# Carrying the fixed instruction order of a sink-window attention kernel through the first four feed-forward steps

## The chip, the cores and the metric

The kernel is one program on one NeuronCore of a Trainium2 chip. The metric is device time in microseconds (us), the median over runs. The engines are named as in the profile: PE (TensorE matmuls), PEld (its weight loads), DVE (VectorE), ACT (ScalarE), POOL (GpSimd) and SP (SyncE, which here only issues DMAs). Each engine works through its own queue in order and waits there for semaphores of the others.

## What is computed

The inputs are q, k, v of shape (2, 8, 768, 64), and two pairs of feed-forward weights, all fp32.

```python
keep = (pos[None, :] < n_sink) | ((rel >= 0) & (rel < window))
a = softmax(where(keep, scale * q @ k.T, -1e9));  x = (a @ v), heads joined: (1536, 512)
h = x @ moe_w_in;   x = softplus(h) @ moe_w_out
h = x @ moe2_w_in;  out = (h * clip(h + 3, 0, 6) / 6) @ moe2_w_out
```

The first feed-forward part is called w1 ("softplus"), the second w2 ("hard"); w_in is 512 x 2048 and w_out 2048 x 512.

## The kernel before

**Attention** (`banded_attention`) handles 12 groups of 128 query rows, each in two quads of four heads. Iteration n is quad n % 2 of group n // 2. In it PE computes the scores `s`; DVE adds the mask and takes the row maximum (`xs`, `mx`, L481); ACT takes the exponential (`P`, L486); PE transposes P (`pt`, L511; the 16 sink columns as `pts`, L502, which POOL has gathered into `PS`, L491); DVE or ACT copies the transposed block to SBUF (`PT`); and PE multiplies with v (`o`, L553, sinks at L538). The second half of a quad's transposes and products is done one iteration later. When both quads of a group are through, DVE takes the reciprocal of the row sums (`rs`, L561 and L562) and scales the output (`x`, `normalise`, L567). PE turns x (`xtr`, `turn_x`, L575), and ACT and DVE write it as a high and a low fp32r part into `xT` (`store_hi` L578, `store_lo` L582). PSUM tile `o` has one buffer.

**Feed-forward** (`Ffn.run`) is a list of 96 steps: (w1, w2) x 3 blocks of 512 tokens x 16 chunks of 128 hidden units. Step s has `stage_a`: 12 matmuls of 128x512 into PSUM tile `h` (L143), then the activation. For w1 that is five ACT instructions, a POOL subtraction `u`, two DVE instructions (L172 and L173), a last ACT copy `g` (L174) and a POOL subtraction (L175). Two steps behind it comes `stage_b`: 12 matmuls that add into the four tiles `y` (L200). The h tiles have three buffers (pool `psa`, shared with the scores), so the products of step s+3 wait until L173 of step s has read its h.

**Weights.** The inputs arrive as 8-byte words, and each 128 x 512 half of a weight chunk must be converted: three DVE instructions (L95, L98, L101), one ACT (L105), one POOL (L106). In the attention the middle value lies in SBUF, in the feed-forward part in a PSUM tile `m`. The 64 halves are taken in a fixed sequence; of w1's 32, HALVES lists the iterations of the attention that end with one conversion (10 of them), and `filler` spreads the other 22 over steps 2 to 14 of the first block. Since step 2 is the first whose activation is not already in the attention code, its filler asks for five halves at once.

**What sets the order.** The tile framework's scheduler chooses the order of each engine's queue from the dependencies. Around the attention loop stands `with in_order(tc)`: it ties every instruction to the one before it on the same engine, in the order of the code. Steps 0 and 1 of w1 are in part written inside that loop: `ffn.products` at n = 24 and 25, `ffn.activate` in the same iterations, and after n = 25 the loop turns and stores the last group. What comes later is free, and the scheduler may put free instructions between the tied ones.

```python
            if NQ <= n < NQ + 2:
                ffn.activate("w1", "softplus", 0, n - NQ, lambda: None)
            if n in HALVES:
                w.half()
```

```python
            if key == first and blk == 0:
                self.w.upto(w0 + ((32 - w0) * (s + 1) + 14) // 15)
```

Of the kernel before, what the change touches and what calls it, by code (L numbers as in the profile page):

```python
# [8 lines left out]
F32 = mybir.dt.float32  # L9
# [5 lines left out]
ALU = mybir.AluOpType  # L15
# [7 lines left out]
SLOTW = P + SK  # L23
SLOTPOS = (0, 2, 1, 3)
TB = 2
HALVES = (5, 7, 9, 11, 13, 15, 17, 19, 21, 23)
WARM = 22


class in_order:  # L30
# [87 lines left out]
class Ffn:  # L118
# [103 lines left out]
    def run(self, specs, out, nblk, w0, pool2):  # L222


        steps = [(key, kind, blk, c) for (key, kind, _, _) in specs for blk in range(nblk) for c in range(16)]
        n = len(steps)
        first = specs[0][0]

        def filler(s):
            key, kind, blk, c = steps[s]  # L230
            if key == first and blk == 0:
                self.w.upto(w0 + ((32 - w0) * (s + 1) + 14) // 15)
            else:
                for _ in range(1 + s % 2):
                    if self.w.coming or self.w.todo:
                        self.w.half()

        for s in range(n + 2):
            if s < n:
                self.stage_a(*steps[s], lambda: filler(s))  # L240
            i = s - 2
            if i < 0 or i == n - 2:
                continue
            key, kind, blk, c = steps[i]
            for j in range(4):
                if i == n - 1:

                    with self.tc.issue_after(last.ins) if j else ExitStack():
                        self.stage_b(*steps[n - 2], j)
                last = self.stage_b(key, kind, blk, c, j)  # L250
# [10 lines left out]
def sink_window_attention_ffn_kernel(  # L261
# [46 lines left out]
    with ExitStack() as body:  # L308
        big = body.enter_context(tc.tile_pool(name="big", bufs=1))
        xT = big.tile([P, 2, 4, NT], F32R, name="xT")  # L310
        w = Weights(nc, body.enter_context(tc.tile_pool(name="wt", bufs=1)), 4)
        NW0 = 8
        wpool0 = body.enter_context(tc.tile_pool(name="wp0", bufs=1))
        psa = body.enter_context(tc.tile_pool(name="psa", bufs=3, space=PSUM))
        ffn = Ffn(tc, xT, w, psa)
        order = [(0, 0)] + [x for c in range(15) for x in ((c + 1, 0), (c, 1))] + [(15, 1)]
        for c, io in order[: 2 * NW0]:
            w.add("w1", c, io, w1_in, w1_out, wpool0)

        ffn.tmp = body.enter_context(tc.tile_pool(name="tmp", bufs=1))  # L320
        with ExitStack() as att:
            banded_attention(att, tc, qT, kT, v, ident, NSv, Wv, xT, psa, ISQ, w, ffn)

        wpool1 = body.enter_context(tc.tile_pool(name="wp1", bufs=1, reuse_waits="tile"))
        ffn.psy = body.enter_context(tc.tile_pool(name="psy", bufs=1, space=PSUM, reuse_waits="tile"))
        w.psum = body.enter_context(tc.tile_pool(name="psw", bufs=1, space=PSUM, reuse_waits="tile"))
        for c, io in order[2 * NW0 :]:
            w.add("w1", c, io, w1_in, w1_out, wpool1)
        w.fetch()
        homes = {x: wpool0 if n < 2 * NW0 else wpool1 for n, x in enumerate(order)}  # L330
        ffn.run(specs, out, NT // 512, w.done, lambda c, io: homes[c, io])


    rv = nc.values_load(near[0:1, 0:1], min_val=0, max_val=1)
    with tc.If(rv < 1):
        nc.scalar.preload_act_table_set("natural_log_exp_and_others")
        with ExitStack() as body:
            big = body.enter_context(tc.tile_pool(name="gbig", bufs=1))
            xT = big.tile([P, 2, 4, NT], F32R, name="gxT")
            with ExitStack() as att:  # L340
                dense_attention(att, tc, qT, kT, v, ident, NSv, Wv, xT, ISQ)
            w = Weights(nc, body.enter_context(tc.tile_pool(name="gwt", bufs=1)), 4)
# [8 lines left out]
            ffn.run(specs, out, NT // 512, 4, lambda c, io: wpool)  # L351


def banded_attention(ctx, tc, qT_d, kT_d, v, ident, NSv, Wv, xT, psa, isq, w, ffn):
# [236 lines left out]
    with in_order(tc):  # L591
        fetch(0)
        z = one.tile([P, 512], BF16, name="z")
        nc.vector.memset(z, 0.0)
        nc.gpsimd.iota(rmc, pattern=[[-1, P]], base=0, channel_multiplier=1, allow_small_or_imprecise_dtypes=True)
        nc.gpsimd.iota(col, pattern=[[1, P]], base=0, channel_multiplier=0, allow_small_or_imprecise_dtypes=True)

        nc.gpsimd.iota(ph, pattern=[[0, 2], [-MAXSINK, 4]], base=4 * MAXSINK, channel_multiplier=1)
        nc.vector.tensor_single_scalar(out=ph, in_=ph, scalar=3 * MAXSINK, op=ALU.bitwise_and)
        nc.vector.tensor_single_scalar(out=owner, in_=ph.rearrange("p a c -> p (a c)"), scalar=0, op=ALU.is_equal)  # L600
        nc.vector.memset(m_one[:, :, P:SLOTW], hid)
        nc.vector.tensor_scalar(out=tB, in0=rmc, scalar1=0.0, scalar2=hid, op0=ALU.is_lt, op1=ALU.mult)
        spare = ps1.tile([P, 512], F32, tag="tr", name="spare")
        keep_busy(WARM)
        masks(0)
        fetch(1)
        fetch_sinks(0)
        fetch(2)
        keep_sinks(0)
        for n in range(NQ + 3):  # L610
            g, quad = divmod(n, 2)
            new, old = n < NQ, 0 <= n - 1 < NQ
            done = (n - 3) // 2 if n % 2 and n >= 3 else None
            if new:
                scores(n)
            if n == NQ:
                ffn.products("w1", 0, 0)
            if done is not None:
                normalise(done)
            if n == NQ + 1:  # L620
                ffn.products("w1", 0, 1)
            if n < 3:
                keep_busy(6)
            if old:
                transposes(n - 1, 1)
                transposes(n - 1, 2)
            if new:
                exps(n, 0)
            if n >= 4 and n % 2 == 0:
                store_lo(n // 2 - 2)  # L630
            if old:
                copies(n - 1, 1)
                copies(n - 1, 2)
                apply_v(n - 1, 0)
            if new:
                exps(n, 1)
                transposes(n, 0)
            if done is not None:
                turn_x(done)
            if old:  # L640
                apply_v(n - 1, 1)
                apply_v(n - 1, 2)
                if n % 2 == 0:
                    inverse((n - 1) // 2)
            if new:
                copies(n, 0)
            if done is not None:
                store_hi(done)
            if quad == 1 and g + 1 < NG:
                keep_sinks(g + 1)  # L650
                if g % NB == 0:
                    own_sinks(g // NB)
                if g == 3:
                    fetch_sinks(1)
                if g + 3 < NG:
                    fetch(g + 3)
                if g == 0:
                    w.fetch()
            if n < 3:
                masks(n + 1)  # L660
# [119 lines left out]
```

## Time and profile before

| what | value |
|---|---|
| runs, device us | 656.67 median of 3 (655.88 to 656.87) |
| profiled execution, device us | 656.36 |
| its span, first to last instruction | 654.5 us, mean granted clock 0.994 |
| PE busy | 637.3 us, 97% of the span |
| DVE, ACT, POOL busy | 337.4, 334.1, 215.0 us |
| chain that ended last | PE 92%, issue 4% |

The profiled execution's own time is 1.9 us more than its span. The attention takes about the first 118 us, the w1 part the stretch to about 380 us, w2 the rest. PE is busy throughout both feed-forward parts; the one long idle stretch of PE lies where the attention ends.

### The profile page before, as it was taken

The page shows a single profiled execution, that of the slowest core. Times are in us where ns is not written, and L with a number is a line of the kernel's source. Part 1 is how long each engine was busy: PE and PEld are TensorE (multiplying, and loading weights), DVE is VectorE, ACT ScalarE, POOL GpSimd, SP SyncE. Part 2 cuts the span into 40 slices and gives each one's busy share as a digit, 9 for nine tenths or more (in the row PEclk, how much of TensorE's full clock was granted, in tenths as well). Part 3 has the DMA queues.
Part 4 walks back from the last instruction along what each step waited for, and adds up shares of the span by engine and source line. Part 5 has one row for each costly group of instructions (what it writes and reads, how often), then busy time and mean ns, then how long its engine had stood idle before and what let it go on. Part 6 is the DMA issues. An engine that isn't in the chain of part 4 may idle for free.

```text
span 654.5 us, 8810 instructions
## 1 busy us (share of the span) xinstructions
PE 637.3 (97%) x3160; PEld 525.3 (80%) x3160; DVE 337.4 (52%) x693; ACT 334.1 (51%) x707; POOL 215.0 (33%) x197
## 2 busy tenths in 40 slices
PE   8999999779999999999999999999999999999996
PEld 4888788668888888888888888888888888888884
DVE  4778987799932412225699999222232222322221
ACT  3767776568775756667688774222222222222221
POOL 1023122388965444444688993000000000000000
PEclk9999999979999999999999999999999999999999
DMA  7835552750000000003565640000010000100001
GB/s 231 259 126 158 163 178 88 246 182 1 1 0 2 0 1 1 2 1 91 179 200 179 212 137 33 1 1 0 2 65 1 1 0 1 64 1 0 1 1 70
DMA packets 38143, 47.07 MB, mean 72 GB/s; under 512 B 2121, under 2 KB 30793, under 8 KB 38089
## 3 DMA queue, kind: packets, MB, share of 16 engines
q1 hardware_dynamic: 37400, 46.15, 22.3%
q8 instruction: 27, 0.44, 0.3%
q10 hardware_dynamic: 688, 0.26, 0.2%
q14 instruction: 28, 0.22, 0.1%
HBM read 43.26 MB, written 3.15 MB: 71 GB/s over the span
## 4 chain that ended last, share of the span: by engine, by line
PE 92%; issue 4%; POOL 1%; ACT 1%; DVE 1%; POOLq 0%; DVEq 0%
PE h_w L143 40%; PE y_w L200 40%; PE o L553 4%; PE s L469 2%; PE pt L511 2%; PE spare L589 2%; PE o L538 1%; POOL w_w L106 1%; PE xtr L575 0%; DVE PT L524 0%; ACT P L486 0%; POOL ring L446 0%; POOL PS L491 0%; PE pts L502 0%; DVE xs L481 0%
## 5 line engine op out<-in xcount | busy, mean ns | idle before, releaser
L143 PE MATMUL h_w<-xT,w_w 128*128 128x512 f32 x1152 | 283.3, 391 | 7.6 <-DVE e_w L173 7.6
L143 PEld LDWEIGHTS h_w<-xT,w_w 128*128 128x128 f32 x1152 | 217.1, 189 | 53.7 <-DVE e_w L173 7.9
L200 PE MATMUL y_w<-g_w,w_w 128*128 128x512 f32 x576 | 142.4, 389 | 0.0
L200 PE MATMUL y_w<-w_w,g_w 128*128 128x512 f32 x576 | 138.9, 389 | 0.0
L200 PEld LDWEIGHTS y_w<-w_w,g_w 128*128 128x128 f32 x576 | 108.0, 188 | 23.2 <-ACT g_w L180 0.4
L200 PEld LDWEIGHTS y_w<-g_w,w_w 128*128 128x128 f32 x576 | 108.1, 188 | 22.5
L106 POOL TENSOR_TENSOR w_w<-t_w,w_w 128x512 fp32r<-128x512 f32 x64 | 83.0, 1297 | 47.0 <-ACT w_w L105 46.6
L179 DVE SCALAR_TENSOR_TENSOR h_w<-e_w,h_w 128x512 f32<-128x512 f32 x48 | 33.4, 695 | 89.0 <-ACT e_w L177 89.0
L177 ACT ACTIVATE e_w<-h_w 128x512 f32<-128x512 f32 x48 | 28.7, 599 | 96.4 <-PE h_w L143 94.6
L175 POOL TENSOR_TENSOR g_w<-e_w,g_w 128x512 fp32r<-128x512 f32 x48 | 62.2, 1297 | 47.1 <-ACT g_w L174 45.6
L181 DVE SCALAR_TENSOR_TENSOR g_w<-h_w,g_w 128x512 fp32r<-128x512 f32 x48 | 33.2, 691 | 83.2 <-ACT g_w L180 83.2
L180 ACT ACTIVATE g_w<-h_w 128x512 fp32r<-128x512 f32 x48 | 28.7, 598 | 90.4 <-PE y_w L200 90.1
L169 POOL TENSOR_TENSOR u_w<-u_w,e_w 128x512 f32<-128x512 f32 x48 | 62.1, 1294 | 31.9 <-ACT u_w L168 31.9
L486 ACT ACTIVATE P<-xs,mx 128x272 f32<-128x272 f32 (+1 forms) x96 | 47.4, 494 | 34.7 <-DVE mx L481 34.6
L172 DVE SCALAR_TENSOR_TENSOR h_w<-h_w,r_w 128x512 f32<-128x512 f32 x48 | 33.4, 697 | 59.0 <-ACT r_w L170 58.7
L173 DVE TENSOR_TENSOR e_w<-h_w,u_w 128x512 f32<-128x512 f32 x48 | 33.0, 688 | 33.9 <-POOL u_w L169 33.7
L165 ACT ACTIVATE e_w<-h_w 128x512 f32<-128x512 f32 x48 | 28.3, 592 | 42.4 <-PE h_w L143 36.3
L105 ACT ACTIVATE w_w<-t_w 128x512 fp32r<-128x512 f32 x64 | 40.1, 626 | 17.9 <-DVE t_w L101 17.2
L553 PE MATMUL o<-v,PT 128*128 128x64 f32 x352 | 45.0, 271 | 1.6 <-DVE PT L524 1.6
L553 PEld LDWEIGHTS o<-v,PT 128*128 128x128 f32 x352 | 42.7, 191 | 2.8 <-DVE PT L524 2.5
L95 DVE TENSOR_SCALAR m_w<-raw_w 128x512 int32<-128x512 int32 x54 | 37.4, 693 | 8.1 <-DMA raw_w<-in_moe_w_in_dram 3.9
L174 ACT ACTIVATE g_w<-e_w 128x512 fp32r<-128x512 f32 x48 | 30.0, 624 | 20.1 <-DVE e_w L173 15.6
(80 smaller groups left out, 523.8 us busy)
## 6 DMA issues: line engine op xcount, KB each, us to landing
raw_w<-in_moe_w_out_dram SPq DMA_DIRECT2D x32, 512.0 KB, 4.4
raw_w<-in_moe_w_in_dram SPq DMA_DIRECT2D x32, 512.0 KB, 4.8
v<-in_v_dram SPq DMA_DIRECT2D x12, 256.0 KB, 5.1
out_dram<-o SPq DMA_DIRECT2D x12, 256.0 KB, 2.1
q<-in_q_dram SPq DMA_DIRECT2D x11, 256.0 KB, 3.5
ring<-in_k_dram SPq DMA_DIRECT2D x11, 256.0 KB, 3.8
ring<-in_k_dram ACTq DMA_DIRECT2D x2, 128.0 KB, 6.1
q<-in_q_dram SPq DMA_DIRECT2D x2, 128.0 KB, 6.0
```

The source lines that it names most:

```text
L95: nc.vector.tensor_scalar(out=m, in0=hi, scalar1=3, scalar2=0x3FFFFFF8, op0=ALU.logical_shift_left, op1=ALU.bitwise_and)
L105: nc.scalar.activation(wt[:, 0, :], t.bitcast(F32), AF.Copy)
L106: nc.gpsimd.tensor_tensor(out=wt[:, 1, :], in0=t.bitcast(F32), in1=wt[:, 0, :].bitcast(F32), op=ALU.subtract)
L143: nc.tensor.matmul(h, wt[:, ws, kk * P : (kk + 1) * P], xT[:, xs, kk, t0 : t0 + 512], start=(n == 0), stop=(n == 11),)
L169: nc.gpsimd.tensor_tensor(out=u, in0=u, in1=e, op=ALU.subtract)
L172: nc.vector.scalar_tensor_tensor(out=h, in0=h, scalar=0.0, in1=r, op0=ALU.max, op1=ALU.add)
L175: nc.gpsimd.tensor_tensor(out=glo, in0=e, in1=ghi.bitcast(F32), op=ALU.subtract)
L179: nc.vector.scalar_tensor_tensor(out=h, in0=e, scalar=6.0, in1=h, op0=ALU.min, op1=ALU.mult)
L181: nc.vector.scalar_tensor_tensor(out=glo, in0=h, scalar=1.0 / 6.0, in1=ghi.bitcast(F32), op0=ALU.mult, op1=ALU.subtract)
L200: ins = nc.tensor.matmul(y, lhsT, rhs, start=(c == 0 and n == 0), stop=(c == 15 and n == 2))
L486: nc.scalar.activation(dst, xs, AF.Exp, scale=-1.0, bias=s["mx"][:, h : h + 1], accum_out=s["sum"][:, h : h + 1])
L553: nc.tensor.matmul(s["o"][:, h, :], t[:, o : o + P], st[gg]["v"][:, h, :], start=(k == 0 and (i <= 1 or hh == 0)), stop=(k == len(blocks) ...
```

## The change

The `in_order` block now also holds steps 0 to 3 of the feed-forward part (FIXED = 4), and their filler does nothing. `run` is cut in two calls, 0 to FIXED inside the block and the rest outside it. Twelve halves are converted in the attention: iterations 20 and 22 are added to HALVES, which then has every iteration from 19 to 23. The other 20 w1 halves are spread over steps 4 to 14. `normalise` and `activate` of the last group and of step 0 now come in iteration 24 (`n == NQ`), with normalise first; step 1's activation moves out of the loop into `run`. The rest of the loop is only indented less. Cut to its core:

```diff
-HALVES = (5, 7, 9, 11, 13, 15, 17, 19, 21, 23)
+HALVES = (5, 7, 9, 11, 13, 15, 17, 19, 20, 21, 22, 23)
+FIXED = 4
...
+    def filler(self, s):
+        key, kind, blk, c = self.steps[s]
+        if s < self.first_free:
+            return
+        if key == self.specs[0][0] and blk == 0:
+            if self.w0 is None:
+                self.w0 = self.w.done
+            n, of = s + 1 - self.first_free, 15 - self.first_free
+            self.w.upto(self.w0 + ((32 - self.w0) * n + of - 1) // of)
...
-        with ExitStack() as att:
-            banded_attention(att, tc, qT, kT, v, ident, NSv, Wv, xT, psa, ISQ, w, ffn)
...
-        ffn.run(specs, out, NT // 512, w.done, lambda c, io: homes[c, io])
+        ffn.begin(specs, out, NT // 512, FIXED, lambda c, io: homes[c, io])
+        with in_order(tc):
+            with ExitStack() as att:
+                banded_attention(att, tc, qT, kT, v, ident, NSv, Wv, xT, psa, ISQ, w, ffn)
...
+            w.fetch()
+            ffn.run(0, FIXED)
+        ffn.run(FIXED, 1000)
...
-            if done is not None:
-                normalise(done)
             if n == NQ + 1:
                 ffn.products("w1", 0, 1)
+            if done is not None and n < NQ:
+                normalise(done)
...
-            if NQ <= n < NQ + 2:
-                ffn.activate("w1", "softplus", 0, n - NQ, lambda: None)
+            if n == NQ:
+                normalise(NG - 1)
+                ffn.activate("w1", "softplus", 0, 0, lambda: None)
```

Line numbers of the changed kernel are larger, by 1 in the feed-forward code and by 12 in the attention. In the rows below, h_w1_0_c is the h tile of step c, y_w1_0_j one of the four y tiles, xtr_11 the turned output of the last group, and the last number of a name is only a counter.

PE, from the products of step 1 on, before:

```order
L143 MATMUL h_w1_0_1_1667<-xT_83,w_w1_1_0_635 128x512 x12
L143 MATMUL h_w1_0_2_1715<-xT_83,w_w1_2_0_896 128x512 x12
L143 MATMUL h_w1_0_3_1808<-xT_83,w_w1_3_0_1112 128x512 x11
L575 MATMUL xtr_11_1680<-ident_59,x_11_1665 128x128 x4
L143 MATMUL h_w1_0_3_1808<-xT_83,w_w1_3_0_1112 128x512
L143 MATMUL h_w1_0_4_1857<-xT_83,w_w1_4_0_1361 128x512 x12
L200 MATMUL y_w1_0_0_1792<-g_w1_0_0_1651,w_w1_0_1_764 128x512 x3
```

and now:

```order
L144 MATMUL h_w1_0_1_1685<-xT_83,w_w1_1_0_635 128x512 x12
L587 MATMUL xtr_11_1698<-ident_59,x_11_1669 128x128 x4
L144 MATMUL h_w1_0_2_1733<-xT_83,w_w1_2_0_896 128x512 x12
L201 MATMUL y_w1_0_0_1760<-g_w1_0_0_1671,w_w1_0_1_764 128x512 x3
L201 MATMUL y_w1_0_1_1764<-g_w1_0_0_1671,w_w1_0_1_764 128x512 x3
L201 MATMUL y_w1_0_2_1768<-g_w1_0_0_1671,w_w1_0_1_764 128x512 x3
L201 MATMUL y_w1_0_3_1772<-g_w1_0_0_1671,w_w1_0_1_764 128x512 x3
L144 MATMUL h_w1_0_3_1776<-xT_83,w_w1_3_0_1112 128x512 x12
L144 MATMUL h_w1_0_4_1815<-xT_83,w_w1_4_0_1361 128x512 x12
```

The turning of the last group moved from behind 35 product matmuls to right behind step 1's, and the y products of step 0 moved ahead of the products of steps 3 and 4. Behind step 4 come y of step 1, the products of step 5, y of step 2 and the products of step 6.

DVE, behind the scaling x of the last group, before (further conversions follow between the third row and the last three, 14 instructions in all):

```order
L567 TENSOR_TENSOR x_11_1665<-o_11_1574,rs_11_1648 128x512
L95 TENSOR_SCALAR m_w1_4_1_1739<-raw_w1_4_1_1240 128x512
L98 SCALAR_TENSOR_TENSOR m_w1_4_1_1739<-raw_w1_4_1_1240,m_w1_4_1_1739 128x512
...
L172 SCALAR_TENSOR_TENSOR h_w1_0_1_1667<-h_w1_0_1_1667,r_w1_0_1_1688 128x512
L101 SCALAR_TENSOR_TENSOR t_w1_6_1_1778<-raw_w1_6_1_1746,m_w1_6_1_1779 128x512
L172 SCALAR_TENSOR_TENSOR h_w1_0_2_1715<-h_w1_0_2_1715,r_w1_0_2_1730 128x512
L173 TENSOR_TENSOR e_w1_0_1_1687<-h_w1_0_1_1667,u_w1_0_1_1689 128x512
L582 TENSOR_TENSOR xT_83<-xtr_11_1680,xT_83 128x4x128
```

and now:

```order
L579 TENSOR_TENSOR x_11_1669<-o_11_1592,rs_11_1666 128x512
L173 SCALAR_TENSOR_TENSOR h_w1_0_0_1632<-h_w1_0_0_1632,r_w1_0_0_1673 128x512
L174 TENSOR_TENSOR e_w1_0_0_1672<-h_w1_0_0_1632,u_w1_0_0_1674 128x512
L594 TENSOR_TENSOR xT_83<-xtr_11_1698,xT_83 128x4x128
L96 TENSOR_SCALAR m_w1_5_1_1839<-raw_w1_5_1_1429 128x512
L99 SCALAR_TENSOR_TENSOR m_w1_5_1_1839<-raw_w1_5_1_1429,m_w1_5_1_1839 128x512
L102 SCALAR_TENSOR_TENSOR t_w1_5_1_1838<-raw_w1_5_1_1429,m_w1_5_1_1839 128x512
L173 SCALAR_TENSOR_TENSOR h_w1_0_1_1685<-h_w1_0_1_1685,r_w1_0_1_1721 128x512
L96 TENSOR_SCALAR m_w1_7_0_1849<-raw_w1_7_0_1497 128x512
L174 TENSOR_TENSOR e_w1_0_1_1720<-h_w1_0_1_1685,u_w1_0_1_1722 128x512
```

Four conversion instructions stand ahead of the read that frees step 1's h tile, where 15 did. From the L594 row to the read that frees step 3's h tile (the L174 row of step 3) there are 28 DVE rows, both included: the store, seven activation instructions and twenty of conversions.

DVE in the attention, between iterations 20 and 21 (x_9 is the scaled output of group 9), before:

```order
L561 TENSOR_SCALAR rs_9_1417<-sum_9_1242 128x8
L562 RECIPROCAL rs_9_1417<-rs_9_1417 128x8
L567 TENSOR_TENSOR x_9_1431<-o_9_1326,rs_9_1417 128x512
L481 ISA xs_21_0_1440,mx_10_1367<-s_21_0_1423,m_even_120 128x272
L481 ISA mx_10_1367 128x1
```

and now:

```order
L573 TENSOR_SCALAR rs_9_1417<-sum_9_1242 128x8
L574 RECIPROCAL rs_9_1417<-rs_9_1417 128x8
L96 TENSOR_SCALAR t_w1_3_1_1422<-raw_w1_3_1_1003 128x512
L99 SCALAR_TENSOR_TENSOR t_w1_3_1_1422<-raw_w1_3_1_1003,t_w1_3_1_1422 128x512
L102 SCALAR_TENSOR_TENSOR t_w1_3_1_1422<-raw_w1_3_1_1003,t_w1_3_1_1422 128x512
L579 TENSOR_TENSOR x_9_1440<-o_9_1326,rs_9_1417 128x512
L493 ISA xs_21_0_1449,mx_10_1367<-s_21_0_1432,m_even_120 128x272
L493 ISA mx_10_1367 128x1
```

A conversion now stands ahead of the scaling and of the next scores; between iterations 22 and 23 it is the same. On SP, the DMAs of two raw halves (6_1 and 8_0) stood ahead of the loads of group 3; they now stand behind the attention's loads, in the order of their use.

## Rows read from the trace of the kernel before

**Rows 1.** The page's engine table, whole span: busy time (share), count.

```profile
PE 637.3 (97%) x3160; PEld 525.3 (80%) x3160; DVE 337.4 (52%) x693; ACT 334.1 (51%) x707; POOL 215.0 (33%) x197
```

**Rows 2.** Stretches: length, busy (count) by engine, granted PE clock, DMA share, GB/s.

```profile
140.00:640.00 500.00, 500.00 (x2208) 414.01 (x2207) 226.96 (x342) 240.37 (x428) 177.43 (x140) 1.00 0.12 39
60.00:80.00 20.00, 18.68 (x153) 15.86 (x153) 18.16 (x64) 14.46 (x50) 5.83 (x8) 1.00 0.55 169
131.00:133.00 2.00, 0.00 (x0) 0.00 (x0) 1.55 (x4) 2.00 (x5) 1.72 (x2) 0.60 0.93 290
121.60:140.00 18.40, 10.83 (x44) 8.61 (x43) 17.09 (x26) 11.11 (x22) 12.63 (x10) 0.81 0.92 310
140.00:180.00 40.00, 40.00 (x178) 33.14 (x177) 37.69 (x58) 32.27 (x59) 36.24 (x30) 1.00 0.01 1
```

**Rows 3.** Timeline of PE: start, length, instructions, idle before and releaser.

```profile
118.39 8.23 PE L143 MATMUL h_w<-xT,w_w 128*128 128x512 f32 x35
...
134.86 4.56 PE L143 MATMUL h_w<-xT,w_w 128*128 128x512 f32 x12 [7.57 <-DVE e_w L173]
```

**Rows 4.** Chain that ended last, 121 to 145: start, us on the chain.

```profile
126.62 0.45 PE xtr L575 x4
...
127.09 0.60 ACT xT L578
...
139.42 5.44 PE y_w L200 x24
```

**Rows 5.** Timeline of DVE where the attention ends.

```profile
120.92 0.68 DVE L567 TENSOR_TENSOR x<-o,rs 128x512 f32<-128x512 f32 x1
...
134.13 0.68 DVE L173 TENSOR_TENSOR e_w<-h_w,u_w 128x512 f32<-128x512 f32 x1
```

**Rows 6.** Timeline in the attention, iterations 20 to 21, several engines.

```profile
97.59 0.20 DVE L562 RECIPROCAL rs<-rs 128x8 f32<-128x8 f32 x1
...
98.32 0.24 POOL L491 COPY PS<-P 128x64 f32<-128x64 f32 x1 [2.22 <-ACT P L486]
98.57 0.69 DVE L567 TENSOR_TENSOR x<-o,rs 128x512 f32<-128x512 f32 x1 [0.78 <-PE s L469]
99.18 0.43 DVE L481 CUSTOM_DVE_ANT_0 xs<-s,m_even 128x272 f32<-128x272 f32 x1
...
99.72 0.52 ACT L486 ACTIVATE P<-xs,mx 128x272 f32<-128x272 f32 x1 [0.98 <-DVE mx L481]
...
100.65 0.19 ACT L486 ACTIVATION_READ_ACCUMULATOR P<-xs,mx 128x1 f32 x1
...
100.82 0.60 PE L511 MATMUL pt<-ident,P 128*128 128x128 f32 x4
...
101.40 0.42 DVE L95 TENSOR_SCALAR t_w<-raw_w 128x512 int32<-128x512 int32 x1
...
102.33 0.31 POOL L491 COPY PS<-P 128x64 f32<-128x64 f32 x1 [3.78 <-ACT P L486]
...
102.58 0.69 DVE L101 SCALAR_TENSOR_TENSOR t_w<-raw_w,t_w 128x512 int32<-128x512 int32 x1
```

**Rows 7.** Timeline of PE, a stall in the attention.

```profile
69.75 0.70 PE L511 MATMUL pt<-ident,P 128*128 128x128 f32 x4 [0.81 <-DVE xT L582]
```

**Rows 8.** The DVE sum L561 by min/median/max ns, its longest, and POOL beside it.

```profile
L561 DVE TENSOR_SCALAR rs<-sum x12: 161/166/720, 18.8 to 116.6; 128x8 f32<-128x8 f32 x12
...
62.87 0.72 DVE L561 TENSOR_SCALAR rs<-sum 128x8 f32<-128x8 f32 x1
...
62.51 1.04 POOL L398 TENSOR_TENSOR vs<-vs,owner 64x512 f32<-64x512 f32 x1
```

**Rows 9.** SP's issue of an early raw half, and PE's first stall in the attention.

```profile
9.20 0.43 SPq L82 DMA_DIRECT2D raw_w<-in_moe_w_out_dram  x1
...
13.34 1.10 PE L553 MATMUL o<-v,PT 128*128 128x64 f32 x8 [0.78 <-DVE PT L524]
```

**Rows 10.** Chain that ended last, 92 to 121: the products of step 1.

```profile
118.46 2.72 PE h_w L143 x11
```

More of the change, by code (lines that the diff above doesn't have):

```diff
@@ L220, in evac, with begin, run @@
             nc.sync.dma_start(out[t0 + j * P : t0 + (j + 1) * P, :], o)
[L222 to L238, printed above, removed]
+    def begin(self, specs, out, nblk, first_free, pool2):
+        self.specs, self.out, self.nblk, self.first_free, self.pool2 = specs, out, nblk, first_free, pool2
+        self.steps = [(key, kind, blk, c) for (key, kind, _, _) in specs for blk in range(nblk) for c in range(16)]
+        self.w0 = None
+    def filler(self, s):
[7 more added lines that the diff above has]
+            self.w.upto(self.w0 + ((32 - self.w0) * n + of - 1) // of)
+        else:
+            for _ in range(1 + s % 2):
+                if self.w.coming or self.w.todo:
+                    self.w.half()
+    def run(self, a, b):
+        n = len(self.steps)
+        for s in range(a, min(b, n + 2)):
             if s < n:
-                self.stage_a(*steps[s], lambda: filler(s))
+                self.stage_a(*self.steps[s], lambda: self.filler(s))
             i = s - 2
@@ L243, in run @@
                 continue
-            key, kind, blk, c = steps[i]
+            key, kind, blk, c = self.steps[i]
             for j in range(4):
@@ L350, in sink_window_attention_ffn_kernel @@
             w.upto(4)
-            ffn.run(specs, out, NT // 512, 4, lambda c, io: wpool)
+            ffn.begin(specs, out, NT // 512, 0, lambda c, io: wpool)
+            ffn.run(0, 1000)
 def banded_attention(ctx, tc, qT_d, kT_d, v, ident, NSv, Wv, xT, psa, isq, w, ffn):
@@ L589, in keep_busy @@
             nc.tensor.matmul(spare, z[:, 0:P], z, start=True, stop=True)
[L591 to L617, printed above, removed]
-            if done is not None:
-                normalise(done)
[L620 to L660, printed above, removed]
-            if NQ <= n < NQ + 2:
-                ffn.activate("w1", "softplus", 0, n - NQ, lambda: None)
-            if n in HALVES:
-                w.half()
@@ new lines, in banded_attention @@
+    fetch(0)
+    z = one.tile([P, 512], BF16, name="z")
+    nc.vector.memset(z, 0.0)
+    nc.gpsimd.iota(rmc, pattern=[[-1, P]], base=0, channel_multiplier=1, allow_small_or_imprecise_dtypes=True)
+    nc.gpsimd.iota(col, pattern=[[1, P]], base=0, channel_multiplier=0, allow_small_or_imprecise_dtypes=True)
+    nc.gpsimd.iota(ph, pattern=[[0, 2], [-MAXSINK, 4]], base=4 * MAXSINK, channel_multiplier=1)
+    nc.vector.tensor_single_scalar(out=ph, in_=ph, scalar=3 * MAXSINK, op=ALU.bitwise_and)
@@ new lines, in banded_attention @@
+    nc.vector.tensor_single_scalar(out=owner, in_=ph.rearrange("p a c -> p (a c)"), scalar=0, op=ALU.is_equal)
+    nc.vector.memset(m_one[:, :, P:SLOTW], hid)
+    nc.vector.tensor_scalar(out=tB, in0=rmc, scalar1=0.0, scalar2=hid, op0=ALU.is_lt, op1=ALU.mult)
+    spare = ps1.tile([P, 512], F32, tag="tr", name="spare")
+    keep_busy(WARM)
+    masks(0)
+    fetch(1)
+    fetch_sinks(0)
+    fetch(2)
+    keep_sinks(0)
+    for n in range(NQ + 3):
+        g, quad = divmod(n, 2)
+        new, old = n < NQ, 0 <= n - 1 < NQ
+        done = (n - 3) // 2 if n % 2 and n >= 3 else None
+        if new:
+            scores(n)
+        if n == NQ:
+            ffn.products("w1", 0, 0)
+        if n == NQ + 1:
+            ffn.products("w1", 0, 1)
+        if done is not None and n < NQ:
+            normalise(done)
+        if n < 3:
+            keep_busy(6)
+        if old:
+            transposes(n - 1, 1)
+            transposes(n - 1, 2)
+        if new:
+            exps(n, 0)
+        if n >= 4 and n % 2 == 0:
+            store_lo(n // 2 - 2)
+        if old:
+            copies(n - 1, 1)
+            copies(n - 1, 2)
+            apply_v(n - 1, 0)
+        if new:
+            exps(n, 1)
+            transposes(n, 0)
+        if done is not None:
+            turn_x(done)
+        if old:
+            apply_v(n - 1, 1)
+            apply_v(n - 1, 2)
+            if n % 2 == 0:
+                inverse((n - 1) // 2)
+        if new:
+            copies(n, 0)
+        if done is not None:
+            store_hi(done)
+        if quad == 1 and g + 1 < NG:
+            keep_sinks(g + 1)
+            if g % NB == 0:
+                own_sinks(g // NB)
+            if g == 3:
+                fetch_sinks(1)
+            if g + 3 < NG:
+                fetch(g + 3)
+            if g == 0:
+                w.fetch()
+        if n < 3:
+            masks(n + 1)
+        if n == NQ:
+            normalise(NG - 1)
+            ffn.activate("w1", "softplus", 0, 0, lambda: None)
+        if n in HALVES:
+            w.half()
```

24 lines of the change are left out of this document (12 added, 12 removed).

## Prediction

> **What bounds the kernel now.** I read the engine table first: PE is busy 97% of the span [rows 1], so time can only be won where PE idles. Then the stretches: from 140 to 640 us PE is busy in all 500 us at a granted clock of 1.00, which is the 2.4 GHz level, and in the attention (60 to 80) it lacks 1.3 us in 20 [rows 2]. So whatever starts the solid stretch earlier or later moves the end by the same amount. The timeline of PE shows one long idle time: 35 products begin at 118.39, and the products of step 4 come at 134.86 after 7.57 us, released by DVE's L173 [rows 3]. That is the L173 of step 1, which frees the h tile (three buffers) that step 4 needs.
>
> Why is it so late? The chain gives it: xtr_11 was turned at 126.62, and ACT's store_hi followed at 127.09 [rows 4]. ACT's order is tied up to there, and step 1's activation stands behind store_hi. But x_11 itself was ready at 121.6 (120.92 + 0.68) [rows 5]; its turning stood behind the 35 products on PE. Meanwhile DVE, free of the tie, took up conversions, so that L173 came only at 134.13 [rows 5].
>
> The idle time has a second price. The granted clock was 0.60 in the mean of 131 to 133, so mostly at the 1.2 GHz level, when PE had been idle for some 4 us [rows 2], and the 12 products behind it took 4.56 us [rows 3], where a product takes 0.227 (5.44 / 24 [rows 4]) and 12 take 2.72. That is 1.84 us more.
>
> **Part by part.**
>
> *A. The old stall.* Turning and store_hi now come right behind step 1's products, and four conversion instructions instead of 15 stand ahead of the freeing read. Forecast: xtr_11 is written when the 12 products end, 2.72 us behind their start at 118.46 [rows 10], so at 121.2 before the shift of B. PE, in its new order, asks for step 4's products after xtr (0.45) and three times 12 matmuls (step 2, y of step 0, step 3): 0.45 + 3 x 2.72 = 8.6 us after step 1's. The freeing read is there after xtr (0.45), store_hi (0.60) [rows 4] and seven DVE instructions, the store included, at some 0.7 us each: 6.0 us. So this wait has 2.6 us of slack and should be gone, with the slow products behind it: 7.57 + 1.84 = 9.41 us removed.
>
> *B. Two more conversions in the attention.* The conversion of an odd iteration runs on DVE from 101.40 to 103.27 (102.58 + 0.69) [rows 6], 1.87 us. The new one starts behind the reciprocal, which ends at 97.79, and ends at 99.66. Before, x started at 98.57 after 0.78 us of idle time [rows 6], which is cover: x is late by 99.66 - 98.57 = 1.09, and so are the masked scores xs behind it (99.18). ACT's exponential had waited 0.98 us for that row, and moves by the same 1.1: the second one's sum, read until 100.84 (100.65 + 0.19), comes at 101.94. PE's third transpose of that quad, in the group at 100.82, stood at about 101.04 and now waits some 0.9 us. A conversion's length behind an exponential has a precedent: at 69.75 PE waited 0.81 us for DVE behind a conversion [rows 7]. PE is nearly solid there [rows 2], so I count it all, twice: **+1.8**. Bounds: 0, if DVE's slack before the next quad takes it up; 3.74, both conversions in full. The value between is taken because the 0.78 idle is in the trace. ACT's copy falls into its own 0.98 idle, POOL's subtraction into waits like 2.22 us [rows 6]; without that cover each would add its length to the next exponential or gather, within the upper bound.
>
> *C. A new wait, step 6's products.* In the new order PE reaches them after step 1's, xtr, steps 2 to 5 and y of steps 0, 1 and 2: 0.45 + 8 x 2.72 = 22.2 us after step 1's start, which B shifts to 118.46 + 1.8 = 120.26. So they are wanted at 142.5. They need the read of step 3's h, the last of 28 DVE rows that begin with the store. That begins when xtr (122.98 to 123.43) and store_hi (0.60) are through, at 124.07. The pace of DVE: 58 instructions in 40 us, 0.69 each, in the solid part, and 26 in 18.4 us, 0.708 each, from 121.6 to 140, where some of its waits are for ACT [rows 2]. The last row starts 27 paces later and takes 0.68: it ends at 143.4 by the first, at 143.9 by the second, so PE waits 0.9 or 1.4. I take **+1.4**, since the stretch is the same one and the activations of steps 1 to 3 wait for ACT in the same way. Bounds: 0, at the 0.65 that independent instructions nearly reach; 2.0, at 0.73, the pace of a conversion's dependent instructions.
>
> *D. The DMAs.* Two raw halves of 0.5 MB leave the early loads, among which SP issued such halves at 9.20; PE's first wait in the attention is 0.78 us, for a copy [rows 9]. The gain is between 0 and that 0.78, and I take 0, since the row names DVE and not a DMA as releaser. The halves are used late and have the whole attention to land; other raw halves come from 118 us on as before, and the first conversions behind store_lo have theirs.
>
> *E. The clock.* PE's granted clock stayed at 1.00 around waits of 0.81 us [rows 2, 7], so the waits of B and C are priced by their length alone. The rest of the program follows PE one to one.
>
> **Sum.** -9.41 + 1.8 + 1.4 = -6.2 us. The profiled execution took 656.36, 0.3 less than the median of 656.67: 650.2 by the first, **650.5 us** by the median.
>
> **A rule weighed.** The row sum L561, 166 ns in the median, once took 0.72 us at 62.87, while POOL worked from 62.51 to 63.55: 0.55 lost, though POOL's copy PS beside a conversion took 0.31 instead of 0.24 [rows 6, 8]. The sum can do without what follows. The Trainium skill, SBUF — State Buffer, section "SBUF: two separate sides", calls the port pair of DVE and GpSimd an exclusive lock: a DVE instruction with two SBUF inputs and a GpSimd instruction that reads SBUF exclude each other for the whole of one of them. By that the gather PS at 98.32 would wait behind the new conversion's second or third instruction. The trace agrees in the L561 row and not in the copy, which lost 0.07 and not most of 0.69.
>
> **Rivals.**
>
> *The attention takes the conversions for nothing* (B is 0). For it: DVE was idle 0.78 and ACT 0.98 at the very place [rows 6]. Against it: 0.78 is less than half of 1.87, and PE has little idle time to hide the rest. The time: 650.5 - 1.8 = 648.7, and 647.3 if the wait of C goes too. Chance 0.12.
>
> *POOL and DVE exclude each other in the new conversions.* The gather PS waits for one DVE instruction in each, 0.69 us, and the sink products behind it with it: 2 x 0.69 = 1.4 more, 651.9. For it stands the L561 row, against it the copy [rows 6, 8]. Chance 0.06.
>
> *The tie doesn't keep conversions out.* Free instructions may still stand between the tied ones, and four do. If the freeing read were as late as with 15, eleven more at 0.69 are 7.6 us, less 2.6 of slack: 5.0 of wait, with the slow clock's 1.84 behind it. -6.2 + 5.0 + 1.84 = +0.6: 657.3. Against it: the order shows four. Chance 0.05.
>
> *DVE becomes the bound of steps 4 to 14*, the side on which it gets slower. The 20 halves left fall on 11 steps, 1.82 each, 5.45 conversion instructions and two of the activation: 7.45 in a step. At 0.69 that is 5.14 us, where PE's 24 matmuls take 5.44 [rows 2, 4]. It decides from 0.73 us an instruction on; the 6.2 us are used up at (5.44 + 6.2 / 11) / 7.45 = 0.81. At 0.83 a step takes 6.18, eleven lose 8.2: 650.5 + 8.2 = 658.7. Against it: from 140 to 180 DVE kept 0.69 beside a solid PE, and was busy 37.69 of 40 us, so it can't run much above that [rows 2]. Chance 0.05.
>
> **How the numbers follow.** The forecast has what is left, 0.72. Its own bounds are, with 1 us of B and 1 of C at a time either way and D's gain, 648 to 653; the first rival reaches 647.3, most of it above 647.8. The range 647.8 to 653.3 holds all of the forecast but its ends, the port rival and most of the first: 0.8. Two tenths of a percent, which is about what a measurement can tell, are 1.3 us: faster than 655.4 are the forecast and the first two rivals, 0.90; the third lies within, 0.05; the fourth is slower, 0.05.
>
> **What would show it.** Right: no wait ahead of step 4's products and no stretch at a low clock near 131; xtr_11 directly behind the products of step 1; these about 1.8 us later than 118.46, with PE waits of about 0.9 at the third transposes of iterations 21 and 23; a wait near 1.4 ahead of step 6's products, released by DVE; PE solid from there on, some 6 us ahead of before. Wrong: waits of PE at steps 7 to 14 released by DVE's reads of h (the fourth rival), a wait of several us at step 4 (the third), or a gap at the end of the attention for a raw half that came late.

## The result, and the profile after

| what | before | after |
|---|---|---|
| runs, device us | 656.77 median (655.88 to 657.08) | 649.79 median (649.69 to 650.26) |
| ratio to before, 95% interval | 1 | 0.9897 (0.988 to 0.9914) |
| span of the profiled execution | 654.5 us | 647.8 us |
| mean granted clock | 0.994 | 0.999 |

The change is 7.0 us faster by the medians and 6.7 by the spans. 650.5 was forecast. The engine table answers to [rows 1]; PE's work is the same, its share is 98% because the span is shorter.

```profile
PE 636.9 (98%) x3159; PEld 524.1 (81%) x3160; DVE 336.0 (52%) x693; ACT 333.9 (52%) x707; POOL 215.8 (33%) x197
```

The timeline of PE of the changed kernel from step 1's products on, to compare with [rows 3] (start, length, instructions, idle time before and its releaser):

```profile
119.95 3.02 PE L144 MATMUL h_w<-xT,w_w 128*128 128x512 f32 x12
122.81 0.60 PE L587 MATMUL xtr<-ident,x 128*128 128x128 f32 x4
123.16 3.00 PE L144 MATMUL h_w<-xT,w_w 128*128 128x512 f32 x12
126.00 2.88 PE L201 MATMUL y_w<-g_w,w_w 128*128 128x512 f32 x12
128.72 5.60 PE L144 MATMUL h_w<-xT,w_w 128*128 128x512 f32 x24
...
139.60 2.88 PE L201 MATMUL y_w<-g_w,w_w 128*128 128x512 f32 x12
143.31 3.04 PE L144 MATMUL h_w<-xT,w_w 128*128 128x512 f32 x12 [0.84 <-DVE e_w L174]
```

The row at 128.72 holds the products of steps 3 and 4 in one piece: the wait of 7.57 us between them is gone. The one at 143.31 has a new wait, ahead of step 6's products. The stretches show both, with the granted clock in the third last column (against 0.60 and 0.81 in [rows 2]):

```profile
120.00:140.00 20.00, 20.00 (x91) 16.57 (x91) 17.09 (x26) 14.98 (x28) 13.38 (x11) 1.00 0.91 316
140.00:160.00 20.00, 19.16 (x84) 15.52 (x84) 19.25 (x31) 16.36 (x31) 18.91 (x16) 1.00 0.00 0
145.00:640.00 495.00, 494.99 (x2183) 409.20 (x2182) 221.72 (x334) 234.55 (x417) 170.61 (x134) 1.00 0.13 39
```

In the attention the timeline of all engines at the first added conversion answers to [rows 6]:

```profile
97.61 0.20 DVE L574 RECIPROCAL rs<-rs 128x8 f32<-128x8 f32 x1
...
98.15 0.69 DVE L99 SCALAR_TENSOR_TENSOR t_w<-raw_w,t_w 128x512 int32<-128x512 int32 x1
...
98.35 0.59 POOL L503 COPY PS<-P 128x64 f32<-128x64 f32 x1 [2.23 <-ACT P L498]
...
99.49 0.68 DVE L579 TENSOR_TENSOR x<-o,rs 128x512 f32<-128x512 f32 x1
...
100.09 0.43 DVE L493 CUSTOM_DVE_ANT_0 xs<-s,m_even 128x272 f32<-128x272 f32 x1
100.24 0.97 PEld L565 LDWEIGHTS o<-v,PT 128*128 128x128 f32 x8 [0.34 <-ACT w_w L106]
100.27 1.08 PE L565 MATMUL o<-v,PT 128*128 128x64 f32 x8
...
101.29 0.94 PE L523 MATMUL pt<-ident,P 128*128 128x128 f32 x4
...
102.07 0.60 PE L587 MATMUL xtr<-ident,x 128*128 128x128 f32 x4
```

and two rows of PE at the same place before, not shown so far:

```profile
99.98 1.00 PE L553 MATMUL o<-v,PT 128*128 128x64 f32 x8
...
101.27 0.60 PE L575 MATMUL xtr<-ident,x 128*128 128x128 f32 x4
```

The scaling x comes at 99.49 instead of 98.57, the scores 0.91 later, and PE reaches xtr 0.80 later. It loses that in two pieces, which the start times give and the idle column hardly does, because each is split into bits: the products into o begin 0.29 later, and by xtr another 0.51 is gone, in the four transposes at 101.29, which take 0.94 instead of 0.60, and just ahead of them. The first has to do with x itself: o has one buffer, and the next group's first product into it waits until x has read it (99.49 + 0.68 = 100.17; PE's load starts at 100.24). The load's releaser is given as ACT's L106, which ended at 100.23; no data of that instruction go into o. That x was meant was tried, in e9 below.

### The profile page after: what moved, and what is told of

Read it like the earlier page. It is cut to its first block, busy times and chain, and to the rows that moved or that the text cites. A ratio compares the mean times of both kernels' runs of the same rounds, so it can differ in the third digit from the quotient of the medians.

```text
span 647.8 us, 8816 instructions
## 1 busy us (share of the span) xinstructions
PE 636.9 (98%) x3159; PEld 524.1 (81%) x3160; DVE 336.0 (52%) x693; ACT 333.9 (52%) x707; POOL 215.8 (33%) x197
## 4 chain that ended last, share of the span: by engine, by line
PE 88%; issue 5%; DVE 3%; ACT 2%; POOL 1%; POOLq 0%; ACTq 0%; DVEq 0%
PE y_w L201 39%; PE h_w L144 39%; PE o L565 3%; PE s L481 2%; PE pt L523 2%; PE spare L601 2%; PE o L550 1%; ACT P L498 1%; POOL w_w L107 1%; DVE xs L493 0%; DVE PT L536 0%; PE xtr L587 0%; DVE t_w L102 0%; DVE e_w L174 0%; POOL ring L458 0%
## 5 line engine op out<-in xcount | busy, mean ns | idle before, releaser
L176 POOL TENSOR_TENSOR g_w<-e_w,g_w 128x512 fp32r<-128x512 f32 x48 | 62.2, 1297 | 45.2 <-ACT g_w L175 45.2
L173 DVE SCALAR_TENSOR_TENSOR h_w<-h_w,r_w 128x512 f32<-128x512 f32 x48 | 33.4, 696 | 58.6 <-ACT r_w L171 58.6
L174 DVE TENSOR_TENSOR e_w<-h_w,u_w 128x512 f32<-128x512 f32 x48 | 33.0, 688 | 28.5 <-POOL u_w L170 28.4
L106 ACT ACTIVATE w_w<-t_w 128x512 fp32r<-128x512 f32 x64 | 40.1, 626 | 12.3 <-DVE t_w L102 11.5
L96 DVE TENSOR_SCALAR m_w<-raw_w 128x512 int32<-128x512 int32 x52 | 36.0, 693 | 7.9 <-DMA raw_w<-in_moe_w_in_dram 3.8
```

The source lines that it names most:

```text
L96: nc.vector.tensor_scalar(out=m, in0=hi, scalar1=3, scalar2=0x3FFFFFF8, op0=ALU.logical_shift_left, op1=ALU.bitwise_and)
L106: nc.scalar.activation(wt[:, 0, :], t.bitcast(F32), AF.Copy)
L173: nc.vector.scalar_tensor_tensor(out=h, in0=h, scalar=0.0, in1=r, op0=ALU.max, op1=ALU.add)
L176: nc.gpsimd.tensor_tensor(out=glo, in0=e, in1=ghi.bitcast(F32), op=ALU.subtract)
```

## The experiments

PE's start differs between profiles: its 22 first matmuls took 6.34 to 7.37 us. So besides medians and ratios I compare the time from PE's first product into o (13.34 us before, 13.36 after) to the end of the span.

| kernel | us, median | ratio to before (95%) | span | first o | first o to end |
|---|---|---|---|---|---|
| before | 656.77 | 1 | 654.5 | 13.34 | 641.16 |
| the change | 649.79 | 0.9897 (0.988 to 0.9914) | 647.8 | 13.36 | 634.44 |
| e1_before12 | 659.09 | 1.003 (1.0018 to 1.0043) | 656.7 | 13.20 | 643.50 |
| e2_after10 | 649.1 | 0.9878 (0.9862 to 0.9895) | 647.3 | 13.87 | 633.43 |
| e3_fixed2 | 650.28 | 0.9902 (0.9885 to 0.9919) | 648.2 | 12.84 | 635.36 |
| e4_late_turn | 655.28 | 0.9976 (0.9967 to 0.9986) | 653.2 | 13.25 | 639.95 |
| e5_filler2 | 648.47 | 0.9881 (0.9859 to 0.9903) | 646.6 | 13.22 | 633.38 |
| e6_filler2_10 | 647.27 | 0.9853 (0.9834 to 0.9872) | 645.4 | 13.56 | 631.84 |
| e7_filler2_9 | 648.07 | 0.9871 (0.9851 to 0.9891) | 645.1 | 13.16 | 631.94 |
| e8_early12 | 649.53 | 0.989 (0.9872 to 0.9909) | 647.7 | 13.17 | 634.53 |
| e9_x_first | 656.57 | 1.0 (0.9985 to 1.0015) | 654.4 | 12.97 | 641.43 |
| e10_turn_only | 655.12 | 0.997 (0.996 to 0.998) | 653.3 | 13.33 | 639.97 |

The ratios stand to runs of the kernel before on the same chip, whose medians were 657.11 for e1 to e4, 657.39 for e5 to e8 and 656.88 for e9 and e10. Between two changed kernels a difference of 1 us lies inside these intervals; there the argument rests on the rows of the profiles, one profile for each kernel.

### Which part of the change removes the old wait

**e1_before12: the conversions alone.** The kernel before with

```diff
-HALVES = (5, 7, 9, 11, 13, 15, 17, 19, 21, 23)
+HALVES = (5, 7, 9, 11, 13, 15, 17, 19, 20, 21, 22, 23)
```

> The kernel before, with the twelve conversion iterations of the change and nothing else. My theory: the number of halves converted early doesn't shorten the old wait, since the free conversions that stand ahead of step 1's freeing read are still 14 instructions; the 7.6 us wait ahead of step 4's products and the slow products behind it stay, and the attention ends 1.6 us later: 656.7 + 1.6 = 658.3 us, slower than before. Rival (the gain of the change comes from the two conversions that it moves out of the crowded place): 6 DVE instructions less there, 4.2 us less wait, 656.7 + 1.6 - 4.2 = 654.1.

Slower than before, and the wait has the same length to the hundredth. PE:

```profile
119.81 8.23 PE L143 MATMUL h_w<-xT,w_w 128*128 128x512 f32 x35
...
136.28 5.36 PE L143 MATMUL h_w<-xT,w_w 128*128 128x512 f32 x12 [7.57 <-DVE e_w L173]
```

The scheduler filled the gap with other conversions: 14 of their instructions stand ahead of step 1's L172 again. Moving two halves into the attention buys nothing there and costs 119.81 - 13.20 = 106.61 against 105.05 from the first o to step 1's products: 1.56 us. The rest of the 2.3 us is the slow clock behind the wait, 5.36 us for 12 products instead of 4.56.

**e10_turn_only: the early scaling and turning alone.** The kernel before with

```diff
-            if done is not None:
+            if done is not None and n < NQ:
                 normalise(done)
...
+            if n == NQ:
+                normalise(NG - 1)
             if NQ <= n < NQ + 2:
```

> The kernel before with one part of the change: the last group is scaled in iteration 24, ahead of step 0's activation, so that it is turned behind 23 products instead of 35; step 2 still asks for five halves, and ten are converted in the attention. My theory: step 1's freeing read comes earlier only by the 12 products, 2.4 to 2.7 us, since the 14 conversion instructions still stand ahead of it; some 5 us of wait and the slow products stay: 654.2. Rival (turning early is the whole gain): 656.7 - 9.4 = 647.3.

```profile
132.66 5.49 PE L143 MATMUL h_w<-xT,w_w 128*128 128x512 f32 x12 [5.35 <-DVE e_w L173]
```

The wait is 2.22 us shorter, and 0.9 of that is given back by the products behind it (5.49 instead of 4.56), so 1.2 us are won from the first o to the end and 1.8 by the median. Not the gain of the change.

**e4_late_turn: the change without the early turning.**

```diff
+        if n == NQ + 1:
+            ffn.products("w1", 0, 2)
+            ffn.products("w1", 0, 3)
         if done is not None:
             turn_x(done)
```

> The changed kernel with one thing undone: the turning of the last group stands behind the products of steps 2 and 3 again (24 products, 5.4 us later), all the rest of the fixed order and the conversions as in the change. My theory: ACT and DVE take up step 1 only behind store_hi, so everything behind it is 5.4 us later, in several waits of 1 to 3 us (y of step 0, products of steps 4 to 6): 649.8 + 5 = 655. Rival (the few conversions ahead of the freeing read are enough): 649.8.

5.5 us slower than the change: the theory's number. The loss is made of several waits of PE and of slow products:

```profile
130.17 2.35 PE L201 MATMUL y_w<-g_w,w_w 128*128 128x512 f32 x9 [0.71 <-DVE xT L594]
134.36 4.61 PE L144 MATMUL h_w<-xT,w_w 128*128 128x512 f32 x12 [1.84 <-DVE e_w L174]
...
148.67 3.03 PE L144 MATMUL h_w<-xT,w_w 128*128 128x512 f32 x12 [1.53 <-DVE e_w L174]
```

So the early turning alone wins 1.2 us, and the rest of the change alone 1.2 as well (641.16 - 639.95, or 2.8 without the 1.54 that its added conversions cost); together they win 6.7. The old wait stood behind two things in a row, xtr and the order of the work behind it (taken apart below), and the clock's price went only when both were undone.

**e3_fixed2: the tie of steps 2 and 3 undone.**

```diff
-FIXED = 4
+FIXED = 2
```

> The changed kernel with FIXED = 2: steps 2 and 3 are free again, and the spread of the 20 halves begins at step 2, with two halves instead of five. xtr_11 then stands behind 11 products of step 2 (2.5 us later than in the change), and eight DVE instructions, not five, stand between the store and step 1's freeing read. My theory: what counts is how early the last group is turned and how much DVE has ahead of that read, not the tie as such: a wait of 1.2 to 1.9 us ahead of step 4's products and a small one at step 6, 650 to 651 us. Rival (without the tie the old wait comes back): 7.6 us of wait and the slow products, about 658.

```profile
132.72 3.06 PE L144 MATMUL h_w<-xT,w_w 128*128 128x512 f32 x12 [1.61 <-DVE e_w L174]
```

The forecast wait came, and the small one forecast at step 6 did not: 0.9 us more than the change. This edit also moves the start of the spread from step 4 to step 2; e5 below has the same spread with steps 2 and 3 tied, and is 2.0 us faster (633.38 against 635.36). So the tie to step 3 is worth 2 us by that pair. Against e10, whose turning is as early, this kernel is 4.6 us faster. Its wait is 3.74 shorter (5.35 and 1.61). Of that, 2.72 is y of step 0, 12 products that PE here has ahead of step 4's and in e10 behind them; 1.01 is the freeing read, which starts 5.94 behind store_hi and in e10 6.95. How much of either comes from two halves asked for at step 2 instead of five, no run separates.

**What stood behind the turning.** The traces show more than the number of conversions. Before the change, ACT, then DVE:

```profile
127.58 1.08 ACT L165 ACTIVATE e_w<-h_w 128x512 f32<-128x512 f32 x2
...
129.58 0.64 ACT L105 ACTIVATE w_w<-t_w 128x512 fp32r<-128x512 f32 x1
...
131.66 1.15 ACT L170 ACTIVATE r_w<-e_w 128x512 f32<-128x512 f32 x2
```

```profile
132.32 0.70 DVE L172 SCALAR_TENSOR_TENSOR h_w<-h_w,r_w 128x512 f32<-128x512 f32 x1 [0.41 <-ACT r_w L170]
...
134.73 0.68 DVE L582 TENSOR_TENSOR xT<-xtr,xT 128x512 fp32r<-128x512 f32 x1
```

and after it, pieces of the chain that ended last:

```profile
124.04 0.50 ACT e_w L166
...
126.44 0.63 ACT r_w L171
```

DVE had done its 14 conversion instructions at 131.91 and stood idle for 0.41 us, for ACT (0.42 in e10, 0.43 in e1). ACT took the activations of steps 1 and 2 in turn, two of each, with a conversion's copy between; in the change it goes through step 1 alone. So the pile on DVE and the order on ACT held step 1 back to about the same time, ACT the longer. From the end of store_hi to the start of the freeing read it is 6.44 us before (127.69 to 134.13) and 4.25 after (124.04 to 128.29), 2.2 less; e4 has 4.23. The turning itself comes 5.2 earlier behind the start of step 1's products (8.06 and 2.86). And PE asks for step 4's products 2.7 later, since y of step 0 now stands ahead of them; in e4 PE waits in these y products for store_lo (the row at 130.17), which came at 134.73 before and comes at 124.07 now. The three are 10.1 us, against the old wait of 7.57 and the 2.5 by which the read is now early. No run takes the pile from DVE and leaves ACT's order as it was, or the reverse.

### The price in the attention

**e2_after10**, the change with the ten iterations of before in HALVES.

> The changed kernel with the ten conversion iterations of before; 22 halves fall on steps 4 to 14. My theory: the two added conversions cost the attention 0.8 us each and buy nothing; step 1's products begin at 118.4 again instead of 119.95, the wait ahead of step 6's products stays near 0.9: 649.8 - 1.6 = 648.2. Rival (the halves that are now late are missed): a new wait for a conversion ahead of steps 6 to 14, 649.8 or more.

```profile
118.90 3.03 PE L144 MATMUL h_w<-xT,w_w 128*128 128x512 f32 x12
...
142.27 3.02 PE L144 MATMUL h_w<-xT,w_w 128*128 128x512 f32 x12 [0.83 <-DVE e_w L174]
```

118.90 - 13.87 = 105.03, as before the change: the whole price of the attention is gone, and the wait at step 6 is unchanged. Only 1.0 of it arrives at the end. From step 6's products to the last y group the profile of this kernel takes 0.52 longer than that of the change (490.28 against 489.76). It is lost between 343 and 384: there the weight loads of y wait three times for POOL's last subtraction of a step (L176), 0.8 us in all, and in the change they don't. Why POOL is late there is not shown; e6, with the same ten iterations, loses nothing of the kind.

**e8_early12**, the extra conversions in iterations 6 and 8:

```diff
-HALVES = (5, 7, 9, 11, 13, 15, 17, 19, 20, 21, 22, 23)
+HALVES = (5, 6, 7, 8, 9, 11, 13, 15, 17, 19, 21, 23)
```

> The changed kernel with the two extra conversions in iterations 6 and 8 instead of 20 and 22. My theory: the price comes from DVE's turn in an even iteration (conversion, then the scaling of the group before, then the scores), wherever it is; step 1's products begin 106.6 us behind PE's first o, as in the change: 649.8. Rival (earlier in the attention DVE has idle time that hides it: it is busy 15.6 of 20 us from 20 to 40): 648.2.

Step 1's products begin at 119.77, 106.60 behind the first o: the same price to a hundredth. An idle share of DVE in a 20 us stretch hides nothing; what stands next in its queue counts.

**e9_x_first**, HALVES as before and

```diff
         if done is not None and n < NQ:
             normalise(done)
+            if n in (NQ - 3, NQ - 1):
+                w.half()
```

> The changed kernel with the two extra conversions one place later on DVE: behind the scaling x of the group before and ahead of the next scores, where they stood ahead of both. In the change PE loses 0.8 us at each, in two waits: the first product into o, for which x must have read the only o buffer (0.3), and the third transpose, for the exponential (0.5). My theory: DVE's place in the queue sets both. The first wait goes, and the scores come 0.84 us later still, so the second grows: 0.5 to 0.8 more at each, 650.8 to 651.5 us. Rivals: the conversion's ACT or POOL part is what delays PE (no change, 649.8), or the o buffer alone is (0.3 less at each, 649.2).

The first part came as the theory has it. Counted from the first o, the product into o stands at 86.66 (before 86.64, change 86.91), so that wait was x's; the next xtr stands at 89.73 (change 88.71), 1.0 later, where 0.5 to 0.8 was expected. That excludes both rivals. But the time rose by 7 us and not by 1 to 1.7. PE, and the stretches behind (granted clock in the third last column):

```profile
101.92 0.94 PE L523 MATMUL pt<-ident,P 128*128 128x128 f32 x4 [1.29 <-ACT P L498]
```

```profile
100.00:104.00 4.00, 2.65 (x20) 2.27 (x20) 3.93 (x13) 3.27 (x12) 1.57 (x2) 0.92 0.00 0
104.00:108.00 4.00, 4.00 (x16) 2.89 (x16) 1.59 (x6) 1.66 (x6) 1.26 (x1) 0.50 0.00 0
...
112.00:116.00 4.00, 4.00 (x16) 2.89 (x16) 1.74 (x4) 0.10 (x1) 0.00 (x0) 0.50 0.00 0
116.00:120.00 4.00, 3.93 (x29) 3.63 (x29) 3.93 (x13) 3.30 (x12) 1.57 (x2) 0.87 0.68 222
```

Behind one wait of 1.29 us the granted clock fell to 0.50, the 1.2 GHz level, and stayed there for some 13 us in which PE was busy without a gap. From this group's xtr to the next one's the profile has 15.98 us (102.70 to 118.68), and that of the change 9.99: 6.0 of the 7.0 us are lost there, 1.0 ahead of it.

### The wait ahead of step 6's products, and a faster kernel

**e5_filler2**, the change with

```diff
-        ffn.begin(specs, out, NT // 512, FIXED, lambda c, io: homes[c, io])
+        ffn.begin(specs, out, NT // 512, 2, lambda c, io: homes[c, io])
```

> The changed kernel with one edit: the spread of the 20 halves begins at step 2, so that steps 2 and 3 have two conversions each, tied in their place ahead of the step's own two DVE instructions. My theory of the wait ahead of step 6's products: it is there because free conversions (20 instructions) pass ahead of step 3's freeing read; with the tied ones 18 DVE rows stand between the store and that read instead of 26, it ends near 138 where PE asks for it at 142.5, and the wait (0.99 us with the loss at its edges, and 0.16 in the products behind it) goes: 649.8 - 1.15 = 648.6. Rival (the same conversions must be done in any case, and the wait only moves to a later step): 649.8.

The wait is gone, and 1.06 us are won from the first o to the end, 1.3 by the median. The read of step 3's h ended at 140.41, not near 138: with no conversion left ahead of step 1's read, DVE waited there 2.31 us for ACT, which the theory had not counted. It was in time all the same. PE, without an idle time:

```profile
139.46 2.88 PE L201 MATMUL y_w<-g_w,w_w 128*128 128x512 f32 x12
142.18 2.88 PE L144 MATMUL h_w<-xT,w_w 128*128 128x512 f32 x12
```

**e6_filler2_10**, the same with the ten iterations of before.

> As e5_filler2, and with the ten conversion iterations of before; 22 halves are spread over steps 2 to 14. My theory: the price of the attention (1.55) and that of step 6 (1.15) are independent, both go: 649.8 - 2.7 = 647.1, give or take 0.5 for the start of the kernel, where PE's first 22 matmuls took between 6.34 and 7.37 us in the profiles so far. Rival (the ten halves don't last until step 6 and PE waits for a conversion): 648.2 or more.

The fastest of all: 647.27 us, 0.9853 of before, 2.6 us below the change from the first o to the end. Both prices go together: 2.60 by the profiles, 2.7 expected. The two single edits won 1.01 and 1.06; the rest is the 0.52 that e2 lost late. PE:

```profile
118.62 3.02 PE L144 MATMUL h_w<-xT,w_w 128*128 128x512 f32 x12
...
140.99 2.88 PE L144 MATMUL h_w<-xT,w_w 128*128 128x512 f32 x12
```

**e7_filler2_9**, e6 without iteration 13 in HALVES.

> As e6_filler2_10, with the conversion of iteration 13 taken out too; 23 halves over 13 steps are 1.77 each, 7.3 DVE instructions or 5.0 us at 0.69, below PE's 5.44. My theory: the wait of 0.81 at the transposes of iteration 14 is that conversion's and goes, nothing else changes: 646.3. Rival (DVE or POOL becomes the bound of steps 2 to 14): 647.1 or more.

A miss. The wait I had put down to that conversion is still there without it, only 0.15 shorter. DVE, then PE:

```profile
67.86 0.44 DVE L493 CUSTOM_DVE_ANT_0 xs<-s,m_one 128x272 f32<-128x272 f32 x1 [1.54 <-PE s L481]
```

```profile
69.42 0.63 PE L523 MATMUL pt<-ident,P 128*128 128x128 f32 x4 [0.66 <-DVE xT L594]
```

DVE itself stood idle for 1.54 us, for the scores, so a conversion in that place is nearly free; the scores and the exponentials behind them take as long without it.

## Why the prediction was right, and where its steps were off

The time (650.5 forecast, 649.79 measured) held, and so did the mechanism in the main: the old stall went, for two smaller prices. Why the old read was late was in part misread, and B and C were both set too high, 0.5 us in all. Point by point:

- **A, the old stall.** Right in its size. Before, step 5's products began at 144.70, 26.3 us behind step 1's at 118.39, where the same 72 matmuls and xtr take 16.8 at the full clock: 9.5 us lost, 9.41 forecast. (The 1.84 in it sets the row's 4.56, which overlaps the next group, against 2.72 from start to start; from start to start, 134.86 to 139.26, it is 1.68.) After, 128.72 shows no gap and the clock is 1.00. The slack was 2.5, 2.6 forecast. The reason given for the late L173, that DVE was busy with conversions, is only half of it: DVE was through with them and waited 0.41 us for ACT, which took steps 1 and 2 in turn. The forecast of six us counted DVE's instructions alone, and they came out near because ACT's five for step 1 take 3.0 us in the new order, where DVE waits for them only 0.27. e4 and e10 show that both parts, the turning and the order behind it, were needed; I had given the sum for them together and said nothing of how it divides.
- **B, the attention.** +1.8 forecast, 1.54 measured (106.59 against 105.05 from the first o). x and the scores came 0.9 later where 1.09 was worked out, because the conversion began at 97.73, before the reciprocal had ended, and its instructions followed more closely. The step that failed is the path: I had PE lose it all at the third transpose. A third of it is the o buffer, which waits for x. And the precedent was no precedent: the wait at 69.75 [rows 7] does not come from the conversion in front of it (e7). The row named store_lo as releaser, and I took what stood before that in the queue for the cause, without looking whether DVE had been waiting there itself.
- **C, the wait at step 6.** Its place and releaser were right, its size was not: +1.4 forecast; 0.84 of idle time, 143.31 - 142.32 = 0.99 from start to start (12 matmuls of 0.227 behind 139.60), 1.15 with the products behind it, which took 0.16 longer to reach the next group. The step that failed is the pace. DVE's rows:

```profile
124.07 0.69 DVE L594 TENSOR_TENSOR xT<-xtr,xT 128x512 fp32r<-128x512 f32 x1 [1.52 <-ACT xT L590]
...
127.08 0.70 DVE L173 SCALAR_TENSOR_TENSOR h_w<-h_w,r_w 128x512 f32<-128x512 f32 x1 [0.27 <-ACT r_w L171]
...
142.58 0.68 DVE L174 TENSOR_TENSOR e_w<-h_w,u_w 128x512 f32<-128x512 f32 x1
```

  27 paces in 18.51 us are 0.686 each, with one wait of 0.27 for ACT. I had both 0.69 and 0.708 and chose the one from the stretch with the waits of the old order; the new order has not got those. 0.69 gave 0.9, the measured idle time nearly. DVE was not alone, though: the read's other input, u, was ready on POOL only at 142.00 (140.70 + 1.30), 0.58 ahead of the read, so fewer conversions on DVE alone would have won at most some 0.6 of the 0.99. In e5 u was ready at 139.42.
- **D, the DMAs.** Zero, as forecast: PE's first product into o came at 13.34 and 13.36.
- **E, the clock.** Right for this kernel: 1.00 around all its waits. But a wait's length is not always its price: e9 adds 1 us to a wait and loses 7.
- **The sum.** -9.5 + 1.54 + 1.15 = -6.8, against 6.7 by the spans and -6.2 forecast.
- **The rivals.** "For nothing" falls by e2 and e8, the tie that lets conversions in by the missing wait at step 4, DVE as the bound by PE's 494.99 of 495 us from 145 to 640. The exclusion of POOL and DVE fits the trace, and cost nothing: PS took 0.59 instead of 0.24 in both added conversions, and ended at 98.94, just behind the conversion's second instruction (98.84). But the sink transposes, which need it, began only at 99.90. The Trainium skill, SBUF — State Buffer, section "SBUF: two separate sides", has one of the two wait for the whole of the other's instruction; this trace agrees in so far as the copy ends with it, 0.35 us late, and the conversion's own instruction kept its 0.69. The prediction held the copy of [rows 6] against that rule, and misread it: that copy started at 102.33, when the conversion's second instruction had 0.22 us left (101.86 + 0.69), and ended 0.09 behind it, so it had no more than that to lose. The L561 row, with a single input, is no case of the rule as the prediction put it.

## What to carry to other kernels

Where an engine waits behind two things in a row, undoing one of them shows little; price them together and test each alone. A tie that keeps optional work out of a stretch doesn't say where that work goes instead: give it fixed places (e5, e6) rather than a ban, or the scheduler puts it ahead of the read that another engine needs. Before a wait in the trace is taken as the price of what stands in front of its releaser, look whether the releasing engine was itself waiting there; that goes for the wait of [rows 7], and for the old wait itself.

## What was not expected of the hardware

Waits of similar length ended very differently for PE's granted clock. Ahead of products it stayed at 1.00 around 0.84 us (the change), 1.61 us (e3) and 1.53 us (e4, the row at 148.67). It fell behind 1.29 us in the attention (e9), for some 13 us, and behind 0.71 and 1.84 us close together (e4), where 12 products took 4.61 us and not 3.03. The same old wait of 7.57 us was followed by 12 products in 4.56 us in one kernel and in 5.36 in another (before, e1), the shorter one of 5.35 us in e10 by 12 in 5.49. What decides it these runs don't show; a short wait of PE has a price that its length doesn't tell.
